# Four-layer linear and segmented attention on one core: the order of the opening, of G's first columns and of the first query loads of each A layer

## The chip, the core and the metric

One NeuronCore of a Trainium2 chip. Its engines run their own instruction queues: TensorE (PE; its weight loads are shown as PEld), VectorE (DVE), ScalarE (ACT), GpSimd (POOL) and SyncE (SP, which here only issues DMAs). The metric is the device time of one execution in microseconds (us); several executions give a median.

## The reference

The input x has 2048 rows of 640 columns (32 heads of 20). Four layers, A, B, A, B, each add to x what they make of its layer norm:

```
A:  q, k, v = x @ wqkv;  pq, pk = phi(q), phi(k)      # phi(t) = t+1 if t>0 else exp(t), + 1e-6
    kv = sum_s pk v^T;  z = sum_s pk                  # per head
    o = (pq kv) / (pq z + 1e-6);  out = o @ wo
B:  four segments of 512 rows, per head: causal softmax attention in the segment,
    mixed by a gate with a read of the memory M, z that the earlier segments left
    out = o @ wo
```

Both A layers use the same weights, and so do both B layers. Everything is float32; the kernel gets it from float16 products by splitting each operand into a high and a low float16 part (three matmuls for each product: high x high, high x low, low x high).

## The kernel before, in words

The 2048 rows go in four segments of 512, each of four tiles of 128 rows; columns go in five chunks of 128 or two halves of 320.

**An A layer in two passes.** The first pass (`g_first`, line 518) goes over the four segments. For each tile it makes the keys (`keys`, line 526: two halves, each 15 matmuls of line 396, then the activation of lines 408 to 411, then two parts at lines 533 and 534 as the tile `pk`), the queries (`queries`, line 542, stored to DRAM as `pqd` by line 546), and, per segment, `memory` (line 549), which adds G = xn^T phi(k): ten products (two halves of columns, five chunks c), each of 12 matmuls of line 560 over the four tiles, evacuated at lines 565 or 567. In segment 0 of the first A layer all keys come first, then memory, then all queries; elsewhere keys and queries alternate.

The last segment ends in `merge` (line 591). It makes the denominators: z summed over partitions by a product with a tile of ones (`square`, line 608; product line 612), `zb` (613) and its reciprocal `rz` (614). It scales G by them (lines 626 to 631), multiplies by the value weight into five tiles `kt` (lines 636 to 657), and these by the output weight into one matrix `wm` (lines 666 to 687). Only then `L["zb"]` is set (between the two, line 661), on which `a_head` (line 714) waits.

The second pass takes three query tiles back at its head: `p_read` (line 697) loads a tile from DRAM (line 701, on SP's queue), multiplies it by `zb` on POOL (703), sums it per head on DVE (706 to 708), scales it on POOL (709). `turn` (line 313) then transposes the tile on PE (320) and copies its high part on ACT (324) and its low part on DVE (325). `a_second` (line 725) multiplies the result by `wm` (line 396 from `o_half`, 465), adds x (`xo`) and feeds the B layer.

**Weights.** `w_prep` (line 228) loads a weight in five chunks into a stage tile (two of these), takes maxima of each chunk on DVE (240), joins them (245, PE 249, 251, PE 255, 258 to 261) into a power-of-two scale, and splits the weight (ACT 265, DVE 266). The query weight's maxima are queued on DVE behind the last lower part that `turn` has issued (`issue_after(self.lower.ins)`).

**The opening** (`opening`, line 1070) starts the first A layer. It normalizes and transposes tile 0, prepares the key weight, then weaves `g_first` with a list of other work: three steps of that list behind each step of segment 0, two behind each step of the later ones. In segment 0 the list is: `others` (transposes of tiles 1 to 3, then their `parts`, line 476), three steps of the query weight, 14 empty steps, the rest of the query weight, and `norms` for segment 1 (its loads, moments and, in `g_norms`, its normalization and eight transposing steps). In segment 1 come the norms of segment 2, then the value and output weights.

**What sets the order.** PE's instructions are issued in the order of the program. Those of the other engines are put in order by a list scheduler, which prefers program order but lets an instruction go ahead when it deems it ready and its engine free; `issue_after` and `high_priority` are the program's means against that. `pause(n)` is n empty steps in a woven list.

**Buffers.** `row` (11 slots of 128 x 640 float32) holds x tiles, normalized tiles, `pk`, `rz`, `kt`, the query tiles read back (`pqi`), their transposes, `xo` and `xn`. There are eight PSUM banks (`bank`).

## Time and profile before

| | |
|---|---|
| median of 3 runs | 1730.26 us (1729.33 to 1732.8) |
| the profiled execution | 1731.61 us, span 1729.8 us |
| PE, DVE, ACT, POOL busy | 95%, 72%, 58%, 31% of the span |
| granted PE clock, mean | 0.992 |
| DMA | 190.89 MB, 110 GB/s over the span |

How to read the profile's lines. A line of the timeline gives the start and the time from first start to last end in us, the engine, the line of the kernel, the operation, the tile written and those read, the shape, the number of instructions merged, and in brackets how long the engine was idle before and who ended it. PE's matmuls overlap each other. A line of the waits gives who waited for whom, the total in us, how often, and the longest. A line of the windows gives a stretch and, for each engine, its busy time and number of instructions, then the granted PE clock as a share of full speed, the busy share of the 16 DMA engines, and GB/s. A line of the chain in order of time gives start, length, and what the time was spent on.

### The profile page before, as it was taken

The numbers are of one execution on the slowest core, as the hardware profiler recorded it, in microseconds if no ns is written. First come the engines' busy times: TensorE is split into PE (matmuls) and PEld (weight loads), VectorE is DVE, ScalarE is ACT, GpSimd is POOL, SyncE is SP. The second block draws the span as 40 slices with busy tenths as digits, with TensorE's granted clock in tenths as the row PEclk, the third lists the DMA queues.
The fourth block names the chain that finished last, engine by engine and source line by source line (L and its number), as shares of the span: only waits on it lengthen the run. The fifth ranks groups of instructions, "written<-read, shape, count | busy, mean of one in ns | idle before, by whom it ended". The sixth has DMA issues, their size and how long they took to land.

```text
span 1729.8 us, 36293 instructions
## 1 busy us (share of the span) xinstructions
PE 1649.9 (95%) x13032; PEld 1032.5 (60%) x13032; DVE 1249.1 (72%) x3966; ACT 997.0 (58%) x1883; POOL 539.3 (31%) x1059
## 2 busy tenths in 40 slices
PE   6999999999999999999999999899999999999998
PEld 4677756554565566556556777566546545645555
DVE  7878785487787677768864457646777877878773
ACT  5666443356657646667675544333675576676673
POOL 3542224032223432333351300321422432233452
PEclk9999999999999999999999999899999999999999
DMA  6424663422322332362211312523232323223432
GB/s 215 141 92 156 220 235 115 137 93 73 105 71 75 104 113 66 124 202 63 82 44 55 99 36 96 199 98 117 73 100 87 113 78 112 94 82 112 133 113 93
DMA packets 110365, 190.89 MB, mean 110 GB/s; under 512 B 14172, under 2 KB 69596, under 8 KB 107624
## 3 DMA queue, kind: packets, MB, share of 16 engines
q1 hardware_dynamic: 97704, 142.68, 25.4%
q0 software_dynamic: 3264, 24.91, 4.0%
q10 hardware_dynamic: 9216, 20.98, 3.1%
q8 instruction: 103, 1.69, 0.4%
q14 instruction: 78, 0.64, 0.1%
HBM read 109.32 MB, written 78.64 MB: 109 GB/s over the span
## 4 chain that ended last, share of the span: by engine, by line
PE 73%; DVE 12%; ACT 7%; POOL 3%; issue 2%; DMA 2%; SPq 0%; ACTq 0%; POOLq 0%; DVEq 0%
PE ps L396 31%; PE ps L382 13%; PE ps L996 7%; PE ps L560 5%; PE ps L320 4%; PE ps L969 4%; PE ps L928 3%; ACT pe L973 3%; DVE ps L934 2%; PE ps L447 2%; PE ps L813 2%; PE ps L1009 1%; DVE wmx L240 1%; DMA pqi<-pqd 1%; PE ps L805 1%
## 5 line engine op out<-in xcount | busy, mean ns | idle before, releaser
L934 DVE CUSTOM_DVE_ANT_0 ps<-ps,maskw 128x384 f32<-128x384 f32 (+3 forms) x1024 | 472.6, 518 | 38.4 <-PE ps L928 35.8
L973 ACT ACTIVATE pe<-ps,lsc 128x512 f32<-128x512 f32 x640 | 397.3, 701 | 75.9 <-PE ps L969 74.6
L396 PEld LDWEIGHTS <-xT 128*128 128x128 f16 x2880 | 281.0, 98 | 112.6 <-issue 7.5
L980 POOL TENSOR_SCALAR_AFFINE_SELECT pe<-pe 128x256 f32<-128x256 f32 (+1 forms) x640 | 229.4, 365 | 370.7 <-ACT pe L973 365.1
L396 PEld LDWEIGHTS <-oT 128*128 128x128 f16 x1920 | 186.1, 98 | 79.7 <-issue 6.4
L996 PE MATMUL ps<-pe,v 128*32 128x512 f32 (+3 forms) x2048 | 165.6, 439 | 12.7 <-POOL pe L980 7.3
L396 PE MATMUL ps<-w_Ak,xT 128*128 128x320 f16 x960 | 140.9, 304 | 2.7 <-ACT w_Ak L265 1.5
L396 PE MATMUL ps<-wm,oT 128*128 128x320 f16 x960 | 142.3, 301 | 1.0
L382 PE MATMUL ps<-xT,w_Bq 128*128 128x512 f16 x600 | 140.3, 379 | 2.8 <-ACT r L420 1.6
L396 PE MATMUL ps<-w_Bo,oT 128*128 128x320 f16 x960 | 141.2, 299 | 1.7 <-ACT oT L324 1.0
L934 DVE DVE_READ_ACCUMULATOR2_ANT mg<- 128x1 f32 x1024 | 142.5, 139 | 0.0
L560 PE MATMUL ps<-pk,xs 128*128 128x321 f16 (+1 forms) x960 | 139.1, 302 | 2.5 <-ACT pk L533 1.6
L382 PE MATMUL ps<-xT,w_Bk 128*128 128x512 f16 x600 | 140.0, 383 | 1.2 <-ACT pe L973 1.2
L396 PE MATMUL ps<-w_Bv,xT 128*128 128x320 f16 x960 | 139.6, 299 | 0.6 <-DVE otok L1016 0.6
L396 PE MATMUL ps<-w_Aq,xT 128*128 128x320 f16 x960 | 137.8, 299 | 0.1
L928 PE MATMUL ps<-ks,qs 60*128 60x512 f16 (+3 forms) x1024 | 122.7, 298 | 6.8 <-ACT pe L973 3.3
L560 PEld LDWEIGHTS <-xs 128*128 128x128 f16 x960 | 93.3, 98 | 40.9 <-issue 3.0
L778 DVE SCALAR_TENSOR_TENSOR nat<-ps,nat 128x512 f16<-128x512 f32 x80 | 55.1, 689 | 82.7 <-ACT nat L777 82.2
L996 PEld LDWEIGHTS ps<-pe,v 128*32 128x32 f32 x2048 | 65.8, 110 | 75.1 <-issue 39.6
L969 PE MATMUL ps<-qs,ks 62*128 62x512 f16 (+3 forms) x1024 | 106.4, 300 | 2.2 <-ACT pe L973 1.1
L411 DVE SCALAR_TENSOR_TENSOR e<-e,r 128x320 f32<-128x320 f32 x128 | 67.7, 529 | 53.1 <-ACT r L410 52.6
L777 ACT ACTIVATE nat<-ps 128x512 f16<-128x512 f32 x80 | 48.4, 606 | 88.0 <-PE ps L382 71.8
(197 smaller groups left out, 2417.7 us busy)
## 6 DMA issues: line engine op xcount, KB each, us to landing
x<-xn ACTq DMA_DIRECT2D x48, 320.0 KB
qs<-qd SPq DMA_DIRECT2D x128, 120.0 KB
ks<-kd SPq DMA_DIRECT2D x128, 120.0 KB
xo<-x SPq DMA_DIRECT2D x48, 320.0 KB
pqi<-pqd SPq DMA_DIRECT2D x32, 320.0 KB
qd<-nat SPq DMA_DIRECT2D x40, 256.0 KB
kd<-nat SPq DMA_DIRECT2D x40, 256.0 KB
x<-in_A_x SPq DMA_DIRECT2D x16, 320.0 KB
```

Of the source, the lines that this page charges most:

```text
L320: nc.tensor.transpose(pt[:, (c - c0) * P:(c - c0 + 1) * P], src[:, c * P:(c + 1) * P], self.ident)
L382: nc.tensor.matmul(p, w[:, c, a, t * P:(t + 1) * P], xT[:, c, b, :], start=k == 0, stop=k == 3 * C - 1)
L396: nc.tensor.matmul(p, xT[:, c, a, i * P:(i + 1) * P], w[:, c, b, n * HN:(n + 1) * HN], start=k == 0, stop=k == 3 * C - 1)
L411: nc.vector.scalar_tensor_tensor(e, e, 1.0, r, op0=OP.min, op1=OP.add)
L560: nc.tensor.matmul(p, xs[:, i, a, c * P:(c + 1) * P], pk[i][:, b, cols], start=k == 0, stop=k == 3 * NT - 1)
L778: nc.vector.scalar_tensor_tensor(nat[:, 1], p, QK_SHIFT, nat[:, 0], op0=OP.mult, op1=OP.subtract)
L928: nc.tensor.matmul(bs[par][:, a:a + n], qs[r, p, i * P:(i + 1) * P], ks[r, p, :n], start=True, stop=True)
L934: nc.vector.tensor_tensor_reduce(bs[par][:, a:a + n], bs[par][:, a:a + n], self.maskw[:, SEG - n:], 1.0, NEG, OP.add, OP.max, G["mg"][:, p ...
L969: nc.tensor.matmul(b[:, a:a + n], ks[r, p, j * P:(j + 1) * P], qs[r, p, j * P:], start=True, stop=True)
L973: nc.scalar.activation(e, b, AF.Exp, scale=self.lsc)
L980: nc.gpsimd.affine_select(d, d, pattern=pat, compare_op=OP.is_ge, fill=0.0, base=0, channel_multiplier=-1)
L996: nc.tensor.matmul(G["pv"][32 * h4:32 * h4 + 32, j * P:], v[j][:, h * E1:h * E1 + 32], G.pop((p, par, j)), start=j == 0, stop=j == 2, skip ...
```

## The change

Six edits.

1. The three tiles that `a_head` reads back for segment 0 of an A layer are loaded as soon as `L["zb"]` is set, which is now right behind the scaling of G; a new key `L["kt"]` is set where `zb` was, and the rest of `p_read` still waits for it.
2. The key weight of layer A is split in two halves of columns, the first half of all five chunks first.
3. Three empty steps stand in front of `others`, and one behind tile 1's transposes, so that both halves of tile 0's keys come before tile 1's transposes on PE, and tile 1's keys before tile 2's; the 14 empty steps become 10, and `g_norms` of segment 1 gets four.
4. The value weight's maxima are queued on DVE behind the last key part issued when its preparation starts (`self.keyed`).
5. In segment 0 of the first A layer, the first two products of G take tiles 0 to 2 first, one behind the other, and tile 3 after that.
6. `square` is filled by POOL instead of DVE.

```diff
-    def w_prep(self, key, stage, w, wait=0, behind=False):
+    def w_prep(self, key, stage, w, wait=0, behind=None):
...
-        with self.tc.issue_after(self.lower.ins) if behind else nullcontext():
+        with self.tc.issue_after(behind.ins) if behind else nullcontext():
...
-        for c in range(C):
-            nc.scalar.activation(w[:, c, 0], st[:, c], AF.Copy, scale=scl)
-            self.last = nc.vector.scalar_tensor_tensor(w[:, c, 1], st[:, c], scl, w[:, c, 0],
-                                                       op0=OP.mult, op1=OP.subtract)
-            if c < C - 1:
-                yield 0.0
+        for cols in (slice(0, HN), slice(HN, D)) if key == ("A", "k") else (slice(0, D),):
+            for c in range(C):
+                nc.scalar.activation(w[:, c, 0, cols], st[:, c, cols], AF.Copy, scale=scl)
+                self.last = nc.vector.scalar_tensor_tensor(w[:, c, 1, cols], st[:, c, cols], scl, w[:, c, 0, cols],
+                                                           op0=OP.mult, op1=OP.subtract)
+                if c < C - 1:
+                    yield 0.0
...
-        yield from self.g_norms(s, box)
+        yield from self.g_norms(s, box, 4 if s == 1 else 0)
...
         xh = self.normed(*m[0])
         yield 0.0
+        yield from pause(wait)
...
+        def product(c, n, tiles, p=None):
+            cols = slice(n * (HN + 1), D + 1 if n else HN + 1)
+            if p is None:
+                p = self.bank()[:, :HN + 1 - n]
+            for i in tiles:
+                for a, b in ((0, 0), (0, 1), (1, 0)):
+                    nc.tensor.matmul(p, xs[:, i, a, c * P:(c + 1) * P], pk[i][:, b, cols],
+                                     start=i == 0 and a == b, stop=i == NT - 1 and a == 1)
+            return p
...
+                    if c == 0:
+                        ahead = 2 if L["early"] and s == 0 and n == 0 else 0
+                        ps = [product(c, n, range(NT - 1)) for c in range(ahead)]
+                    if c < ahead:
+                        p = product(c, n, range(NT - 1, NT), ps[c])
+                    else:
+                        p = product(c, n, range(NT))
...
-        nc.vector.memset(square, 1.0)
+        nc.gpsimd.memset(square, 1.0)
...
+        L["zb"] = zb
         for _ in memory:
             pass
         yield from filled(1)
...
-        L["zb"] = zb
+        L["kt"] = True
...
+    def p_load(self, L, s, i):
         pq = self.row("pqi")
         self.q_pqi.dma_start(pq, L["pqd"][s][i])
+        return pq
+
+    def p_read(self, L, s, i, o, pq=None):
+        nc = self.nc
+        if pq is None:
+            pq = self.p_load(L, s, i)
...
-        box.update(o=[], oT=[self.new_oT()])
+        box.update(o=[], oT=[])
+        pq = [None] * 3
+        if L["kt"] is None:
+            pq = [self.p_load(L, s, i) for i in range(3)]
+        while L["kt"] is None:
+            yield 0.0
+        box["oT"].append(self.new_oT())
         for i in range(3):
-            yield from self.p_read(L, s, i, box["o"])
+            yield from self.p_read(L, s, i, box["o"], pq[i])
...
-                                   key == ("A", "q"))
+                                   {("A", "q"): self.lower, ("A", "v"): self.keyed}.get(key))
...
             xh = [first]
+            yield from pause(3)
             for i in range(1, NT):
                 xh.append(self.normed(*m[i - 1]))
                 yield from self.turn(xh[i], cur[1], i)
+                if i == 1:
+                    yield 0.0
...
-                aux = chain(o, islice(q, 3), pause(14), q, self.norms(src, 1, nxt, 6))
+                aux = chain(o, islice(q, 3), pause(10), q, self.norms(src, 1, nxt, 6))
```

More of the change, by code (lines that the diff above doesn't have):

```diff
@@ L496, in load_segment, with g_norms @@
         yield 0.0
-    def g_norms(self, s, box):
+    def g_norms(self, s, box, wait=0):
         m = box[0]
@@ L515, in g_begin @@
         pqd = [self.dr.tile([NT, P, D], F32, name=f"pqd{n}_{s}") for s in range(NSEG)]
-        return dict(z=z, G=None, pqd=pqd, zb=None, wm=None, early=n == 0)
+        return dict(z=z, G=None, pqd=pqd, zb=None, kt=None, wm=None, early=n == 0)
     def g_first(self, s, box, w, L, behind=None):
@@ L555, in memory @@
                 for c in range(C):
-                    p = self.bank()[:, :HN + 1 - n]
-                    k = 0
-                    for i in range(NT):
-                        for a, b in ((0, 0), (0, 1), (1, 0)):
-                            nc.tensor.matmul(p, xs[:, i, a, c * P:(c + 1) * P], pk[i][:, b, cols],
-                                             start=k == 0, stop=k == 3 * NT - 1)
-                            k += 1
+                    if c == 0:
[5 more added lines that the diff above has]
+                        p = product(c, n, range(NT))
                     g = L["G"][c][:, cols]
@@ L695, in masked @@
         return mem
-    def p_read(self, L, s, i, o):
-        nc = self.nc
+    def p_load(self, L, s, i):
         pq = self.row("pqi")
         self.q_pqi.dma_start(pq, L["pqd"][s][i])
+        return pq
[3 more added lines that the diff above has]
+            pq = self.p_load(L, s, i)
         with self.tc.issue_after(L["split"].ins):
@@ L1098, in last @@
             yield 0.0
+        self.lower = self.keyed = None
         cur = [None, self.x_t(), self.xs_t(0)]
```

## The prediction

> **What bounds the kernel now.** I read the page first, for the shares of engines and of the chain that ended last; then TensorE's (PE's) waits by stage; then busy time in windows.
>
> ```profile
> span 1729.8 us, 36293 instructions
> PE 1649.9 (95%) x13032; PEld 1032.5 (60%) x13032; DVE 1249.1 (72%) x3966; ACT 997.0 (58%) x1883; POOL 539.3 (31%) x1059
> PE 73%; DVE 12%; ACT 7%; POOL 3%; issue 2%; DMA 2%; SPq 0%; ACTq 0%; POOLq 0%; DVEq 0%
> ```
>
> PE is idle for only 80 us. The edits lie in three places that hold part of it: the opening (0 to 66 us), the first head (222 to 263) and the second head (1082 to 1114). The windows show whether time won there is kept (stretch, length; PE, PEld, DVE, ACT, POOL busy with counts; granted PE clock, DMA share, GB/s).
>
> ```profile
> 67.00:118.00 51.00, 51.00 (x381) 37.40 (x379) 40.20 (x91) 38.59 (x76) 30.41 (x49) 1.00 0.24 79
> 165.00:214.00 49.00, 49.00 (x360) 34.92 (x358) 37.95 (x76) 26.37 (x49) 11.00 (x15) 1.00 0.53 192
> 1120.00:1147.00 27.00, 27.00 (x206) 20.41 (x205) 16.20 (x42) 9.11 (x20) 9.91 (x9) 1.00 0.26 86
> ```
>
> Behind the opening and behind the second head PE never rests, at full clock, so a gain there shifts all that follows. I count such gains in full.
>
> **The opening.** The keys of segment 0:
>
> ```profile
> 15.84 3.26 DVE L266 SCALAR_TENSOR_TENSOR w_Ak<-stage,scl_Ak,w_Ak 128x640 f16<-128x640 f32 x4
> 16.76 3.09 PE L396 MATMUL ps<-w_Ak,xT 128*128 128x320 f16 x11 [0.50 <-DVE w_Ak L266]
> 23.41 3.73 PE L396 MATMUL ps<-w_Ak,xT 128*128 128x320 f16 x15
> 27.89 12.39 PE L396 MATMUL ps<-w_Ak,xT 128*128 128x320 f16 x90
> 20.00:28.00 8.00, 5.74 (x31) 4.01 (x30) 4.57 (x15) 6.34 (x14) 6.59 (x13) 0.79 0.91 317
> 28.00:40.20 12.20, 12.20 (x92) 8.78 (x90) 12.03 (x22) 7.08 (x17) 4.19 (x5) 1.00 0.47 163
> 40.20:45.50 5.30, 2.89 (x17) 1.63 (x16) 5.30 (x11) 2.95 (x6) 3.17 (x3) 0.89 0.00 0
> ```
>
> The first half key (15 matmuls) crawls behind the weight's split and ends at 19.85; the second starts at 23.41, behind transposes; the other six are the 90. Split in column halves, the five pieces that the first half key needs take DVE 5 x 0.41 instead of 5 x 0.82 (3.26 / 4), and it ends some 2 us sooner. DVE's total stays (at worst each of five extra starts costs 0.1). With three pauses ahead of the transposes the second half follows at once and ends where its weight does, near 20 instead of 27.1. Then tile 1's transposes and their copies, say 3 us; the 90 matmuls start near 23 instead of 27.89 and, with ten transposes (1.1 us) and some waits for copies among them, end near 37.5 instead of 40.28.
>
> But the last two rows say that from 28 on the limit is DVE: 17.33 of 17.50 us busy. Part of that is work that nothing needs yet:
>
> ```profile
> 36.08 0.14 DVE L245 TENSOR_REDUCE wm<-wmx 128x1 f32<-128x5 f32 x1
> 36.14 0.80 DVE L240 TENSOR_REDUCE wmx<-stage 128x1 f32<-128x640 f32 x1
> 37.83 1.53 DVE L240 TENSOR_REDUCE wmx<-stage 128x1 f32<-128x640 f32 x2
> 40.15 1.53 DVE L240 TENSOR_REDUCE wmx<-stage 128x1 f32<-128x640 f32 x2
> 42.67 0.14 DVE L245 TENSOR_REDUCE wm<-wmx 128x1 f32<-128x5 f32 x1
> 43.17 2.17 DVE L534 SCALAR_TENSOR_TENSOR pk<-e,k_scl,pk 128x320 f16<-128x320 f32 x2
> ```
>
> The first L245 closes the maxima of the query weight. The five L240 behind it and the second L245 are the value weight's, whose program place is in segment 1. They are 0.80 + 1.53 + 1.53 + 0.14 = **4.0 us** between the last keys' steps. The edit pins the maxima behind a key of segment 1, where DVE has 10.8 us free of 51 (row 67 to 118). If that cover fails, the value weight's transpose on PE waits, by at most these 4.0.
>
> So the last key part, at 45.3 now, can be ready at 41.3, if PE's last key matmul ends 2.6 us earlier (two ACT reads, L411, L533, L534, about 0.5 each), at 38.7; 37.5 does. DVE's idle time before 28 (row 20 to 28: 8.00 - 4.57 = 3.4 us) may be filled as well, for 0 to 3 us more; I take none.
>
> G then follows.
>
> ```profile
> PE ps L560 <- ACT pk L533: 1.6, 1, 1.6
> PE ps L560 <- DVE pk L534: 0.8, 1, 0.8
> 45.50:54.00 8.50, 7.83 (x49) 5.01 (x48) 7.02 (x17) 3.71 (x5) 0.48 (x1) 0.87 0.06 25
> 61.16 5.07 PE L560 MATMUL ps<-pk,xs 128*128 128x320 f16 x36
> ```
>
> PE does nine matmuls of G, then waits twice for tile 3's parts. With two columns over three tiles it has eighteen ahead of that point: 9 x 0.14 (5.07 / 36) = **1.3 us** moved into the wait, or the wait gone. The idle time also costs clock: 0.87 over 8.5 us is **1.1 us**, saved if PE doesn't stop. A second PSUM bank is held meanwhile, of eight.
>
> The Trainium skill ("TensorE: Matmul & The Clock Gate", Part 1) says that an idle window of about 3.4 us halves the clock and about 3.4 us of steady work restores it. That agrees with the 0.87 here and, below, with 0.50 behind 7.2 us of idle time; by it the order of the opening could as well keep PE cold, which is rival D.
>
> One wait is left ahead of the queries, PE's transposes of segment 1 behind their normalization.
>
> ```profile
> 55.33 0.77 PE L320 MATMUL ps<-ident,xh 128*128 128x128 f32 x5 [2.00 <-ACT xh L369]
> 66.07 16.46 PE L396 MATMUL ps<-w_Aq,xT 128*128 128x320 f16 x120
> ```
>
> PE and DVE both arrive sooner; the four pauses put one and a third columns (12 x 0.14 each, 2.2 us) in front. Between minus 1 and plus 2 us; I take 0, since G's evacuations and the query weight's split still stand ahead of it on DVE. Sum of the opening: 4.0 + 1.3 + 1.1 = **6.4 us**, bounds 2.5 (ACT and DVE hold each other up, and only the two PE terms stay) and 9.
>
> **The second head.**
>
> ```profile
> 1064.13 26.32 SPq L546 DMA_DIRECT2D pqd<-e  x4
> 1090.62 2.16 SPq L701 DMA_DIRECT2D pqi<-pqd  x4
> 1091.13 11.06 DMA pqi<-pqd
> pqd<-e POOLq DMA_DIRECT2D x32, 160.0 KB, 2.5
> L706 DVE TENSOR_REDUCE rca<-pqi x32: 753/808/821, 257.2 to 1437.4; 128x32 f32<-128x640 f32 x32
> 1070.00:1082.00 12.00, 12.00 (x90) 8.54 (x89) 12.00 (x27) 2.53 (x6) 0.16 (x1) 1.00 0.01 1
> 1091.00:1101.00 10.00, 9.71 (x75) 3.91 (x73) 4.79 (x13) 4.61 (x12) 1.25 (x2) 1.00 1.00 406
> PE ps L320 <- POOL pqi L709: 7.2, 1, 7.2
> 1107.90:1110.10 2.20, 2.15 (x9) 1.72 (x10) 0.68 (x2) 0.81 (x2) 2.20 (x2) 0.50 0.94 401
> 1110.10:1113.50 3.40, 3.40 (x17) 2.12 (x16) 1.58 (x3) 0.49 (x1) 1.75 (x2) 0.61 0.32 136
> ```
>
> The query tiles are read back behind the last query store in SP's queue, at 1090.6, just when two weight fetches fill the DMA engines (share 1.00), and take up to 11 us. PE finishes its product at 1100.7 and stands 7.2 us, to 1107.9. The edit lets the loads go once the denominators are there. They depend on nothing but rows of the pool: of 11, four key parts and rz are held, six are free. SP has only a store to wait for, and the DMA engines are idle (share 0.01). So they go between 1069 and 1087, ahead of the fetches, and land in about 3 us each (an estimate: the 160 KB stores took a median of 2.5). POOL then has three multiplications, DVE three sums (0.8 each; it is idle for 5 of the 10 us from 1091), POOL three scalings, all done by 1100. What is late next is the transposed copy: PE's transposes at 1100.7, ACT and DVE about 1 us, partly beside other transposes; I charge 0.9. Gain 7.2 - 0.9, plus the clock: 2.20 x 0.50 + 3.40 x 0.39 = 2.4. **8.7 us**, bounds 5 and 10.
>
> **The first head.**
>
> ```profile
> 245.65 1.81 SPq L701 DMA_DIRECT2D pqi<-pqd  x4
> 252.37 0.62 DVE L656 TENSOR_TENSOR kt<-ke,kt 128x160 f16<-128x160 f32 x1 [2.31 <-ACT kt L655]
> 262.80 0.55 PE L320 MATMUL ps<-ident,pqi 128*128 128x128 f32 x3 [1.06 <-POOL pqi L709]
> PE ps L612 <- DVE square L608: 1.1, 1, 1.1
> 222.00:237.00 15.00, 14.13 (x104) 9.94 (x103) 15.00 (x34) 5.67 (x10) 0.22 (x1) 1.00 0.22 83
> ```
>
> Here DVE sets the pace (15.00 of 15.00). Earlier loads let the three sums fill its 2.31 us gap, so PE's 1.06 wait and some 0.4 ahead of it go: **1.5 us**, bounds -1 and 3. The memset that moves to POOL frees 0.17 us of DVE and lets PE go 1.1 sooner, but DVE is busy then, so that is counted at nothing; POOL, idle there, hides it. Later heads load as before.
>
> **The sum.** 6.4 + 8.7 + 1.5 = 16.6 us. The profiled execution took 1731.6 (span 1729.8 and 1.8 around it), 1.3 above the median of 1730.26; from that median the forecast is **1714 us**.
>
> **Rivals.** A, the opening yields its 2.5: ACT and DVE pass each half key to and fro, in order, and both were busy already (ACT 6.34 of 8.00 from 20 to 28). 1730.3 - 2.5 - 10.2 = 1718. For it: the ten halves of the key weight add starts on ACT; against it: 4.0 us of DVE work leave. B, the sums slip ahead on DVE in the stretch where it is full (1070 to 1082): 3 x (0.8 + 0.5) = 3.9 us late, 1 covered, so the second head yields 5.8 and the first loses 0.5: 1730.3 - 6.4 - 5.8 + 0.5 = 1718.6. Against it: their program place is still behind the product's inputs. C, the loads stay behind the stores in SP's queue, so the change doesn't do what it says: both heads yield nothing, 1724. With A too, 1728. For it: in the first row of the second head SP sits 26 us on four stores; against it: it does so waiting for data that the loads don't need. D, slower: every gap in the reordered opening keeps PE at half clock. From 21 to 41 some 114 matmuls (90 and the two columns' 24) would take 0.14 more each, 16 us, and the 96 of G behind them 13.4. The opening then loses 29.4 - 6.4 = 23, the heads win 10.2: 1743. If the clock recovers at 41 it is 1730; from about 49 on it is slower than before by over 0.2%. Against it: the stretch from 28 to 40 ran at 1.00 with PE less pressed.
>
> **Chances.** Forecast 0.57, A 0.17, B 0.12, C 0.07, A with C 0.03, D 0.04. Range 1707 (opening 9, second head 10, first 3, and 1 for the spread of runs) to 1723 (A with B); about 0.14 is left out. 0.2% is 3.5 us, about what a measurement of this kernel can tell from no change. Faster by more: the first four, 0.93; within: 0.03; slower: 0.04.
>
> **What would show it.** Right: the value weight's L240 after 80 us; last key part near 41; queries' first matmul near 60 instead of 66.07; pqi loads before the weight fetch, PE's wait for L709 under 1 us, clock 1.00 after it. Wrong: granted clock 0.5 between 25 and 45; DVE sums of pqi before 1082; SP's loads still behind the last store.

## The result and the profile after

Side by side on one chip, the changed kernel took 1722.64 us (median of 5 runs, 1720.99 to 1722.82), the kernel before 1729.33 (1728.34 to 1732.8): ratio 0.9957, 95% interval 0.9942 to 0.9971. On another occasion it took 1721.79 against 1730.68: 0.9954, interval 0.9938 to 0.9970. The change wins 7 to 9 us; the forecast was 16.6. The time lies just inside the forecast's range (1707 to 1723), but that end of it stood for A with B, and B, the late sums of the second head, did not come: that it lies inside is luck.

The page of the changed kernel, span, engines and the chain by engine:

```profile
span 1719.3 us, 36302 instructions
PE 1645.4 (96%) x13032; PEld 1028.9 (60%) x13032; DVE 1250.5 (73%) x3969; ACT 994.2 (58%) x1888; POOL 539.3 (31%) x1061
PE 69%; DVE 15%; ACT 8%; issue 3%; DMA 3%; POOL 2%; SPq 1%; ACTq 0%; DVEq 0%; POOLq 0%
```

PE is idle for 74 us instead of 80, and DVE's share of the chain has risen from 12 to 15%, which points to waits for DVE in place of some of what was won.

I then compared the start of the same matmul in both traces, from the first to the last. PE's lead over the kernel before, in us, in the profiled execution and in that of a repeat (r_after, below):

| place | forecast | measured | repeat |
|---|---|---|---|
| in G, where the kernel before turns to segment 1's transposes (48.7 us) | | 4.4 | 3.6 |
| queries' first matmul (63.4 us) | 6.4 | 2.7 | 1.9 |
| after 150 us | 6.4 | 0.9 | 0.1 |
| behind the first head | 7.9 | 2.4 | 1.7 |
| ahead of the second head (1090 us) | 7.9 | 3.8 | 1.7 |
| behind the second head (1114 us of the kernel before) | 16.6 | 13.0 | 10.8 |
| end | 16.6 | 10.5 | 9.8 |

So the second head gave 9.2 (8.7 forecast). At the first the lead grows by 1.5 and 1.7 (1.5 forecast), but the experiments don't bear this out as the work of edit 1. Of the opening's 6.4, 0.9 and 0.1 were left at 150 us. What else comes and goes, after the heads, are mostly lulls at half clock, told of at the end.

The second head in the changed kernel: SP's and PE's rows, then windows.

```profile
1062.75 1.35 SPq L712 DMA_DIRECT2D pqi<-pqd  x3
1084.44 2.78 SPq L548 DMA_DIRECT2D pqd<-e  x2
```
```profile
1096.80 1.09 PE L321 MATMUL ps<-ident,pqi 128*128 128x128 f32 x8
```
```profile
1091.00:1101.00 10.00, 9.82 (x76) 5.19 (x75) 8.34 (x23) 4.45 (x12) 5.83 (x5) 1.00 0.86 316
1101.00:1114.00 13.00, 13.00 (x100) 9.80 (x99) 8.57 (x25) 4.00 (x9) 2.39 (x3) 1.00 0.62 210
```

Three loads go at 1062.75, ahead of the last stores and of the weights (1090.62 before). PE's transposes of `pqi` start at 1096.80 with nothing waited for; between 1000 and 1130 us the profile lists no wait of PE at all. From 1101 to 1114 it is busy for all 13.00 at clock 1.00.

The opening in the changed kernel, DVE and POOL (an idle time and its releaser stand in brackets):

```profile
33.04 1.40 POOL L479 TENSOR_TENSOR xs<-xh,xs 128x640 f16<-128x640 f32 x1
33.05 1.73 DVE L536 SCALAR_TENSOR_TENSOR pk<-e,k_scl,pk 128x320 f16<-128x320 f32 x1
34.70 2.98 DVE L240 TENSOR_REDUCE wmx<-stage 128x1 f32<-128x640 f32 x4
41.99 0.73 DVE L536 SCALAR_TENSOR_TENSOR pk<-e,k_scl,pk 128x320 f16<-128x320 f32 x1 [0.43 <-ACT pk L535]
42.90 0.49 DVE L412 SCALAR_TENSOR_TENSOR e<-e,r 128x320 f32<-128x320 f32 x1 [0.18 <-ACT r L411]
44.02 0.72 DVE L536 SCALAR_TENSOR_TENSOR pk<-e,k_scl,pk 128x320 f16<-128x320 f32 x1 [0.63 <-ACT pk L535]
```

The four L240 are the query weight's; the value weight's are gone from here, to 96 to 109 us. Yet the last key part ends at 44.02 + 0.72 = 44.7 instead of 45.3: 0.6 earlier, not 4. It was not PE that held it back: PE's last key matmul ended at 38.4, before the 38.7 that the forecast asked for. DVE now stands idle between the last steps, waiting for ACT, and one earlier step lasts 1.73 us, beside a subtraction on POOL. Behind that step it is the other way round: the four maxima run in a row, and ACT waits 2.79 us for DVE's next sum (L412):

```profile
38.12 0.56 ACT L535 ACTIVATE pk<-e,k_scl 128x320 f16<-128x320 f32 x1 [2.79 <-DVE e L412]
```

### The profile page after: what moved, and what is told of

It reads as the page before. It is cut to its first block, busy times and chain, and to the rows that moved or that the text cites. A ratio compares the mean times of both kernels' runs of the same rounds, so it can differ in the third digit from the quotient of the medians.

```text
span 1719.3 us, 36302 instructions
## 1 busy us (share of the span) xinstructions
PE 1645.4 (96%) x13032; PEld 1028.9 (60%) x13032; DVE 1250.5 (73%) x3969; ACT 994.2 (58%) x1888; POOL 539.3 (31%) x1061
## 3 DMA queue, kind: packets, MB, share of 16 engines
q8 instruction: 103, 1.69, 0.4%
## 4 chain that ended last, share of the span: by engine, by line
PE 69%; DVE 15%; ACT 8%; issue 3%; DMA 3%; POOL 2%; SPq 1%; ACTq 0%; DVEq 0%; POOLq 0%
PE ps L397 28%; PE ps L383 13%; PE ps L1020 7%; PE ps L557 4%; PE ps L993 4%; PE ps L952 3%; ACT pe L997 3%; PE ps L321 3%; DVE ps L958 2%; PE ps L448 2%; PE ps L837 2%; PE ps L1033 1%; DVE wmx L240 1%; DVE split L267 1%; DVE st L340 1%
## 5 line engine op out<-in xcount | busy, mean ns | idle before, releaser
L557 PE MATMUL ps<-pk,xs 128*128 128x321 f16 (+1 forms) x960 | 138.7, 301 | 1.4 <-DVE pk L536 1.4
L557 PEld LDWEIGHTS <-xs 128*128 128x128 f16 x960 | 93.3, 98 | 39.6 <-POOL z L541 1.8
L412 DVE SCALAR_TENSOR_TENSOR e<-e,r 128x320 f32<-128x320 f32 x128 | 67.8, 530 | 51.0 <-ACT r L411 50.6
```

Source lines behind the costliest of these rows:

```text
L412: nc.vector.scalar_tensor_tensor(e, e, 1.0, r, op0=OP.min, op1=OP.add)
L557: nc.tensor.matmul(p, xs[:, i, a, c * P:(c + 1) * P], pk[i][:, b, cols], start=i == 0 and a == b, stop=i == NT - 1 and a == 1)
```

## The experiments

Fourteen kernels ran, in four lots, each with the kernel before beside it (1730.02 to 1730.68 us). My theory: the heads do what was forecast, and the opening's gain is lost in DVE's queue, first in the keys, then near 149 us. The rival: the opening wins nothing on PE in the first place.

| kernel | median us | ratio to before, interval |
|---|---|---|
| r_after: the change again | 1721.79 | 0.9954 [0.9938, 0.9970] |
| e1_heads: edit 1 alone | 1720.67 | 0.9948 [0.9934, 0.9963] |
| e2_opening: edits 2 to 5 alone | 1730.32 | 0.9999 [0.9989, 1.0008] |
| e6_vmax: edit 4 alone | 1730.69 | 1.0002 [0.9992, 1.0012] |
| e3_square: change without edit 6 | 1722.58 | 0.9952 [0.9936, 0.9967] |
| e8_nopin: change without edit 4's hold | 1720.17 | 0.9942 [0.9928, 0.9956] |
| e4_casts | 1727.34 | 0.9983 [0.9974, 0.9992] |
| e5_parts (leaves work out) | 1718.55 | 0.9931 [0.9917, 0.9945] |
| e7_pins | 1723.07 | 0.9959 [0.9944, 0.9973] |
| e9_late | 1726.74 | 0.9978 [0.9969, 0.9987] |
| e10_round | 1718.56 | 0.9932 [0.9920, 0.9944] |
| e11_both | 1724.37 | 0.9966 [0.9954, 0.9977] |
| e12_roundnp | 1717.17 | 0.9922 [0.9909, 0.9935] |
| e13_rnpsq | 1717.06 | 0.9925 [0.9913, 0.9937] |

### Heads and opening apart

e1_heads is the kernel before with the early loads alone:

```diff
+        if L["kt"] is None:
+            pq = [self.p_load(L, s, i) for i in range(3)]
```

> Only the early loads of the query tiles, on the kernel before. Theory 1 (the two heads give what was worked out, the opening next to nothing): first head 1.5 us, second 9.0, so PE is 10.5 ahead behind the second head and the time is 1718.5 to 1721. Theory 2 (the heads' gain is partly given back later, and the opening carries part of the whole): the time is 1723 to 1725, well above that of the whole change (1722.6).

e2_opening is the change with the loads and the place of `square` put back.

```diff
-        if L["kt"] is None:
-            pq = [self.p_load(L, s, i) for i in range(3)]
...
-        nc.gpsimd.memset(square, 1.0)
+        nc.vector.memset(square, 1.0)
```

> The opening's edits alone (2 to 5), without the early loads and the moved memset. Theory 1 (the gain is eaten where DVE stops in order for the constants that are loaded behind the value weight): PE is some 2.7 us ahead at the first queries, under 1.2 ahead at 160 us, and the time is 1728 to 1729.5. Theory 2 (the gain at the queries is kept): PE is 2.7 ahead from there to the end, 1726.6.

Edit 1 alone is 9.4 us faster than before, the opening's edits alone nothing: 0.2 us slower, between 1.9 faster and 1.4 slower. So the whole measured gain of the change is that of edit 1. In e2's trace PE is 3.2 us ahead at the queries and 1.5 at 189 us: the rival falls, the gain is there and is lost.

The heads in e1's trace: the second gives 9.2, the first takes 0.4 away, while e2_opening, without the early loads, gains 1.2 there. So theory 1 has its time, but its 1.5 for the first head isn't shown. Of PE's waits there, the one for the scaled tiles (first row, the kernel before) is gone in e1_heads, and one for their transposed copy has come (second row); PE's waits for the parts `xT` of the scaled G grew from 1.6 to 2.7.

```profile
PE ps L320 <- POOL pqi L709: 1.5, 2, 1.1
```
```profile
PE ps L396 <- DVE oT L325: 0.9, 1, 0.9
```

### The value weight's maxima alone

```diff
-                                   key == ("A", "q"))
+                                   {("A", "q"): self.lower, ("A", "v"): self.keyed}.get(key))
```

> The kernel before with one part of the change alone: the maxima of the value weight held behind a key of segment 1. If the prediction's term is right (4.0 us of DVE work stand between the last keys' steps), the last key part comes at 41 to 42 us instead of 45.3, and the time falls by 3 to 4. If DVE's steps there end at the pace of what feeds them (PE's last key matmul at 40.28, ACT's copies of it), the last key part moves by no more than 1 us, DVE shows idle time in its place, and the time falls by no more than 1.

The last key part came at 43.1 + 0.7 = 43.8 us, 1.5 earlier than before, and the time did not fall. DVE in e6_vmax:

```profile
39.05 0.72 DVE L534 SCALAR_TENSOR_TENSOR pk<-e,k_scl,pk 128x320 f16<-128x320 f32 x1 [0.64 <-ACT pk L533]
39.96 0.49 DVE L411 SCALAR_TENSOR_TENSOR e<-e,r 128x320 f32<-128x320 f32 x1 [0.18 <-ACT r L410]
41.08 0.72 DVE L534 SCALAR_TENSOR_TENSOR pk<-e,k_scl,pk 128x320 f16<-128x320 f32 x1 [0.63 <-ACT pk L533]
41.99 0.49 DVE L411 SCALAR_TENSOR_TENSOR e<-e,r 128x320 f32<-128x320 f32 x1
43.12 0.72 DVE L534 SCALAR_TENSOR_TENSOR pk<-e,k_scl,pk 128x320 f16<-128x320 f32 x1 [0.23 <-ACT pk L533]
```

and ACT beside it:

```profile
40.48 0.56 ACT L533 ACTIVATE pk<-e,k_scl 128x320 f16<-128x320 f32 x1 [0.64 <-DVE e L411]
40.95 0.51 ACT L408 ACTIVATE e<-ps,inv_Ak 128x320 f32<-128x320 f32 x1
41.36 0.52 ACT L410 ACTIVATE r<-ps,inv_Ak 128x320 f32<-128x320 f32 x1
42.52 0.57 ACT L533 ACTIVATE pk<-e,k_scl 128x320 f16<-128x320 f32 x1 [0.64 <-DVE e L411]
```

This is a round: ACT reads (L408, L410), DVE adds (L411), ACT writes the part (L533), DVE its low part (L534). ACT's next two reads stand behind its L533, and that waits for DVE. So each half key takes 2.03 us (39.05, 41.08, 43.12), and each engine waits for the other. DVE steps that leave such a round become idle time of DVE: it was busy for 17.33 of 17.50 us before, but the maxima filled gaps that would have been there without them. Two executions of one kernel can differ in when the keys start (by 0.8 us between the change and its repeat), so I also count from the start of the first low part on DVE. From there the last key part is ready after 22.8 us in the kernel before (in e1_heads too) and after 21.0 here. So the forecast's 4.0 was worth 1.8 here and, as e8_nopin shows below, 0.5 in the changed kernel.

### POOL beside DVE

e5_parts is the change with the low parts of the normalized tiles of segment 0 filled with zeros, so it leaves out four subtractions on POOL and what they add to G:

```diff
-        self.nc.gpsimd.tensor_tensor(xs[:, i, 1], xh, xs[:, i, 0], op=OP.subtract)
+        if early:
+            self.nc.gpsimd.memset(xs[:, i, 1], 0.0)
+        else:
+            self.nc.gpsimd.tensor_tensor(xs[:, i, 1], xh, xs[:, i, 0], op=OP.subtract)
```

> The whole change, but in segment 0 the low parts of the normalized tiles (line 479) are filled with zeros by POOL instead of being subtracted: that part of the computation is left out. Theory 1 (DVE's two-input steps run slow beside POOL's subtractions, 1.73 us instead of 0.55): the steps of line 536 take under 0.7 each, and the last key part of segment 0 is ready near 42 instead of 44.7. Theory 2 (the loss is ACT and DVE waiting for each other in turn): it stays at 44 or later. The time by theory 1 is 1 to 2.7 below that of the whole change if nothing eats it, the same if the stop for the constants does.

The groups of the keys' low parts between 20 and 45.5 us, in the change and in e5_parts (busy, mean ns, idle before):

```profile
L536 DVE SCALAR_TENSOR_TENSOR pk<-e,k_scl,pk 128x320 f16<-128x320 f32 x8 | 7.5, 952 | 1.1 <-ACT pk L535 1.1
```
```profile
L539 DVE SCALAR_TENSOR_TENSOR pk<-e,k_scl,pk 128x320 f16<-128x320 f32 x8 | 5.3, 678 | 1.1 <-ACT pk L538 1.1
```

Without the subtractions the eight steps cost 2.2 us less, and nearly all of it is two steps that stand beside a subtraction in the change: 1.56 and 1.73 us, here 0.55 each. (In the kernel before the eight cost 5.7; no low part there stands beside a subtraction, so it is the reordered opening that brought them together.) One step still takes 1.16, beside POOL's sum of z. The last key part came at 42.9 and the queries start at 61.54, each 1.8 us earlier than in the change, which is theory 1's side; of PE's lead of 4.5 at the queries, 2.4 is left at 217 us. The Trainium skill ("SBUF — State Buffer", Who interferes with whom) says that a VectorE instruction with two inputs in SBUF and a GpSimd instruction that reads SBUF can't run side by side: the second waits for the first to end. The trace agrees: in the changed kernel's rows POOL starts at 33.04 and ends at 34.44, DVE's 33.05 ends at 34.78, 0.34 behind it.

### The loss at 149 us

In the changed kernel PE has this wait between 100 and 200 us, which the kernel before has not:

```profile
PE ps L397 <- DVE xT L326: 1.3, 1, 1.3
PE ps L255 <- DVE rs L344: 0.2, 1, 0.2
```

The rows of DVE ahead of it, and of SP:

```profile
133.21 0.23 DVE L184 CAST maskw<-cst 128x128 bf16<-128x128 f32 x1 [4.62 <-DMA cst<-in_const]
147.59 1.53 DVE L240 TENSOR_REDUCE wmx<-stage 128x1 f32<-128x640 f32 x2
149.44 0.88 DVE L326 TENSOR_TENSOR xT<-ps,xT 128x256 f16<-128x256 f32 x2
```
```profile
126.03 0.33 SPq L272 DMA_DIRECT2D wd_Av<-split  x1
126.41 0.42 SPq L182 DMA_DIRECT2D cst<-in_const  x1
133.93 2.23 SPq L236 DMA_DIRECT2D stage<-in_B_wv  x5
```

First I took the casts of the constants, for which DVE waits 4.62 us, and put them on POOL:

```diff
-        nc.vector.tensor_copy(self.maskw[:, SEG - P:], t[:, :P])
-        nc.vector.tensor_copy(self.blk, t[:, P:])
+        nc.gpsimd.tensor_copy(self.maskw[:, SEG - P:], t[:, :P])
+        nc.gpsimd.tensor_copy(self.blk, t[:, P:])
```

> The whole change, but the two casts of the late constants (lines 184 and 185) run on POOL, so that DVE doesn't stand for their load. Theory 1: PE's wait of 1.3 us for the lower part of a transposed tile near 148 us goes, PE stays 2.4 or more ahead up to 214 us, and the time is about 1.4 below that of the whole change, 1721.2. Theory 2 (the wait comes from DVE's load of work, not from the stop): the wait stays and the time is 1722.6.

Both theories fell: PE's wait rose to 2.6 us, and DVE stood at the next load instead. The median is 5.5 above r_after's; the profiled execution, itself faster than that median, has PE 1.5 us behind the kernel before at 217 us. The rest isn't explained.

```profile
148.26 1.64 DVE L240 TENSOR_REDUCE wmx<-stage 128x1 f32<-128x640 f32 x2 [2.47 <-DMA stage<-in_B_wq]
150.21 0.88 DVE L326 TENSOR_TENSOR xT<-ps,xT 128x256 f16<-128x256 f32 x2
```

So I took the order: layer B's maxima stand ahead of L326 in DVE's queue. e7_pins holds all later maxima behind the same key.

```diff
-                                   {("A", "q"): self.lower, ("A", "v"): self.keyed}.get(key))
+                                   self.lower if key == ("A", "q") else self.keyed)
```

> The change with the maxima of all later weights held behind the same key of segment 1, by which the maxima of B's value and query weights stand behind the low parts of the transposed tiles in DVE's queue instead of ahead of them. Theory (the opening's lead is eaten at 149 us because those maxima, one of which waits for a DMA that lands near 148 us, stand ahead of a copy that PE needs): the 1.3 us wait at 149 us goes, PE keeps its lead of 2.6 up to 217 us, and the time is 1 to 2 below the changed kernel's. Rival (DVE's work from 133 to 160 us is too much in total, whatever its order): the wait stays at 1 or more, or another wait for DVE of that length takes its place, and the time stays within 0.5.

The wait for L326 went, and another came: PE's scale of a weight, behind maxima that now come late (at 112 to 115 us, with half clock behind it). PE was 2.1 us behind the kernel before at 136 us. This is the rival's other wait; the median is 1.3 above r_after's, with overlapping intervals.

```profile
PE ps L255 <- DVE wm L251: 3.2, 1, 3.2
```

Both misses said that the late weights are one chain, and that the place to look is where it starts. The value weight's low parts on DVE are written to DRAM (`wd_Av`), the constants' load stands behind that write in SP's queue, and their cast frees the stage buffer for layer B's value weight. e8_nopin gives up the hold of edit 4 and keeps the rest:

```diff
-                                   {("A", "q"): self.lower, ("A", "v"): self.keyed}.get(key))
+                                   self.lower if key == ("A", "q") else None)
```

> The change without the part that holds the value weight's maxima behind a key of segment 1. Theory (the maxima, moved to 96 to 109 us, delay the value weight's low parts on DVE, and by that its write to DRAM, the constants' load behind it in SP's queue, and the later weights, so that DVE comes late to a transposed tile at 149 us): the constants' load is issued before 124 us instead of 126.4, and PE's 1.3 us wait at 149 us falls under 0.5; the last key part comes about 1.5 us later than in the changed kernel, the queries' first matmul likewise, and the time stays within 1 of it. Rival (the late weights' chain does not hang on the maxima): the constants' load stays at 126 us or later, the 1.3 stays, and the time rises by 1.5.

```profile
123.50 0.33 SPq L272 DMA_DIRECT2D wd_Av<-split  x1
123.88 0.42 SPq L182 DMA_DIRECT2D cst<-in_const  x1
131.40 2.24 SPq L236 DMA_DIRECT2D stage<-in_B_wv  x5
```

The wait is gone, and PE keeps the lead that it has at the queries: 2.1 us there and 2.1 at 217 us. The median is 1.6 below r_after's, but the intervals overlap. The last key part came at 44.3 + 0.7 = 45.0 us. Counted from the first low part it takes 21.2 us, and 20.7 in all seven profiles that have the change's keys with the hold: 0.5 later, where I had expected 1.5. Over the kernels that leave the order from the queries to 149 us as it is:

| kernel | queries' first matmul | constants' load | between | PE's wait at 149 | PE's lead at 217 us |
|---|---|---|---|---|---|
| before | 66.07 | 125.83 | 59.8 | none | |
| e1_heads | 65.72 | 125.53 | 59.8 | none | 0.4 |
| e8_nopin | 63.97 | 123.88 | 59.9 | none | 2.1 |
| e12_roundnp | 61.52 | 121.30 | 59.8 | none | 4.6 |
| e13_rnpsq | 59.90 | 119.78 | 59.9 | none | 6.1 |
| e6_vmax (held) | 64.33 | 127.39 | 63.1 | 1.3 | 0.0 |
| the change (held) | 63.38 | 126.41 | 63.0 | 1.3 | 0.9 |
| the change again (held) | 64.17 | 127.28 | 63.1 | 1.3 | 0.1 |
| e3_square (held) | 63.19 | 126.22 | 63.0 | 1.3 | 0.9 |
| e2_opening (held) | 62.85 | 125.88 | 63.0 | 1.3 | 1.5 |
| e5_parts (held) | 61.54 | 124.65 | 63.1 | 1.6 | 2.4 |
| e10_round (held) | 60.99 | 124.29 | 63.3 | 1.3 | 3.0 |

With the hold the constants come 63 us behind the queries, without it 60, whatever else is changed. The hold moves the chain by 3.2 us against PE, and PE then stands for it once, near 149 us.

e9_late sets the constants free of that chain instead:

```diff
-                aux = chain(self.norms(src, 2, nxt, 6), a("v"), a("o"), late())
+                aux = chain(self.norms(src, 2, nxt, 6), late(), a("v"), a("o"))
...
+        with self.tc.issue_after(self.keyed.ins):
+            nc.vector.tensor_copy(self.maskw[:, SEG - P:], t[:, :P])
+            nc.vector.tensor_copy(self.blk, t[:, P:])
```

> The change with the constants' load and casts ahead of the value weight's preparation in segment 1, their casts on DVE held behind a key of that segment, so that the load is not behind the value weight's write in SP's queue and the later weights take a stage buffer that frees at about 126 us instead of 133.9. Theory (the chain through the constants' load eats the opening's lead at 149 us): B's value weight is loaded by 128 us instead of 133.9, PE's 1.3 us wait at 149 us falls under 0.5, PE's lead of 2.6 is kept to 217 us, and the time is 1 to 1.7 below the changed kernel's. Rival (DVE's total of work sets the time there): a wait of PE for DVE of 1 us or more stays between 130 and 217 us, and the time stays within 0.5.

The wait at 149 us is gone and B's value weight loads from 128.14 us, as the theory said, but the lead and the time did not come. The output weight of layer A now takes its stage buffer late (its loads go at 96.39 us, in the change near 60), PE waits for its maxima, at 108 to 112 us with half clock from 111, and is 3.9 us behind the kernel before up to 217 us. Its rows, of SP and of PE's waits:

```profile
96.39 2.24 SPq L237 DMA_DIRECT2D stage<-in_A_wo  x5
```
```profile
PE ps L250 <- DVE wm L246: 4.0, 1, 4.0
```

### The keys' round, and both together

e10_round issues each key part one half key later in segment 0, so that ACT's next reads stand ahead of it:

```diff
                 e = self.phi_a(self.proj_n(xT, w("k"), i, n), self.inv["A", "k"])
-                nc.scalar.activation(pk[i][:, 0, c], e, AF.Copy, scale=self.k_scl)
-                self.keyed = nc.vector.scalar_tensor_tensor(pk[i][:, 1, c], e, self.k_scl, pk[i][:, 0, c],
-                                                            op0=OP.mult, op1=OP.subtract)
+                flush()
+                pend.append((pk[i], c, e))
+                if s or not L["early"]:
+                    flush()
```

> The change with the key parts of segment 0 issued one half key later, so that in ACT's queue the two reads of the next half stand ahead of the part that waits for DVE. Theory (in the tail of the keys the limit is a round of ACT, DVE, ACT, DVE, 2.03 us for each half key, with DVE idle 1.2 of it, which is why 4.0 us taken off DVE brought 1.5): the steps between the last key parts fall from 2.03 to about 1.6, the last key part comes 1 to 2 us earlier than 44.0, and the queries' first matmul by about as much; by the loss at 149 us little of it is kept, and the time stays within 1. Rival (DVE's amount of work sets the tail): DVE stays idle no less, or the last key part stays within 0.4.

The last key part came at 42.6 + 0.7 = 43.3, 1.4 earlier than in the change, and the queries at 60.99, 2.4 earlier (2.1 and 3.1 counted from the first low part). ACT's fifth part, the row of the change that waited 2.79 us, in e10_round:

```profile
36.66 0.56 ACT L530 ACTIVATE pk<-e,k_scl 128x320 f16<-128x320 f32 x1 [1.12 <-DVE e L412]
```

The last key part came as I had said, but not by my theory, and the median fell by 3.2 against r_after's, more than the 1 that I had allowed (the intervals just overlap). Counted from the first low part, this fifth part stands at 14.1 us in the change, 12.0 here and 11.4 in e5_parts; from it to the end of the last low part, all three take 6.6 to 6.7. So all that was won in the keys was won ahead of the fifth part. There the low part that took 1.73 us beside the subtraction, in front of the query weight's maxima, now comes behind them and takes 0.54 (the mean of the eight falls from 952 to 738 ns; one still stands beside a subtraction, 1.55). The round of the last parts as a whole got no shorter: the steps between ACT's last four parts are 1.54, 1.69 and 2.13 us, in the change 0.88, 2.40 and 2.02. (The 1.2 us in that expectation is DVE's busy time in a round, 0.72 + 0.49; it is idle for 0.8.) At 149 us 1.3 was lost again, as expected.

e11_both joins e9's and e10's edits, with `square` back on DVE.

```diff
+                flush()
...
+                aux = chain(self.norms(src, 2, nxt, 6), late(), a("v"), a("o"))
...
+        nc.vector.memset(square, 1.0)
```

> The three edits together on the change: the constants ahead of the value weight, the key parts one half later, and the memset of square back on DVE. If each does what its theory says, PE is 4 to 5 us ahead of the kernel before at the queries and keeps 3.5 or more of it to 217 us, the second head gives its 9, and the time is 2 to 4 below the changed kernel's. If the lulls and DVE's load take it back, the time stays within 1 of the changed kernel's.

It missed: PE was 5.8 us ahead at the queries, then waited 4.4 us for the output weight's maxima, as in e9_late, and was 1.2 behind at 136 us.

e12_roundnp joins the two that worked, e10's edit and e8's, and keeps `square` on POOL.

> The change with the key parts of segment 0 issued one half key later and without the hold on the value weight's maxima. Theory (the round and the delayed weights' chain are the whole loss of the opening): the queries' first matmul comes 4 to 5 us earlier than in the kernel before, PE keeps all of it to 217 us (no wait for the transposed tile at 149 us above 0.3), and the time is 4 to 5 below the changed kernel's, near 1717. Rival (a third limit, DVE's load from 67 to 217 us, takes back any lead above 2): the lead at 217 us is again 2 to 3, with a new wait of PE for DVE between, and the time is that of the change with the key parts alone, 1718.6, or above.

PE is 4.6 us ahead at the queries, and 4.6 at 217 us, with no wait for DVE's transposed tile between: the hold is the whole loss between these two points. e13_rnpsq, with the same opening, has 6.2 and 6.1; no half-clock window falls into its G, and one does in e12_roundnp (50.7 us). 1717.17 us is 4.6 below the repeated change; the two intervals (to 0.9935, from 0.9938) don't overlap. And the value weight's maxima are back among the last keys, where nothing is lost by them. DVE in e12_roundnp:

```profile
38.87 0.55 DVE L531 SCALAR_TENSOR_TENSOR pk<-e,k_scl,pk 128x320 f16<-128x320 f32 x1
39.33 0.81 DVE L240 TENSOR_REDUCE wmx<-stage 128x1 f32<-128x640 f32 x1
40.06 0.54 DVE L531 SCALAR_TENSOR_TENSOR pk<-e,k_scl,pk 128x320 f16<-128x320 f32 x1
41.12 0.80 DVE L240 TENSOR_REDUCE wmx<-stage 128x1 f32<-128x640 f32 x1
41.85 0.53 DVE L531 SCALAR_TENSOR_TENSOR pk<-e,k_scl,pk 128x320 f16<-128x320 f32 x1
```

The last key part is done at 42.4 us (44.7 in the changed kernel), with two of the five maxima between these steps and a third just ahead of them, at 37.74.

### The memset, and the change again

```diff
-        nc.gpsimd.memset(square, 1.0)
+        nc.vector.memset(square, 1.0)
```

> The changed kernel again, unedited, as the base for the others and for a second look at its lulls. Theory (the mechanisms give about 7 to 10 us below the kernel before, the half-clock windows scatter it by 2 to 3): a time of 1720 to 1723, the last key part again at 44 to 45 us, the wait of PE's L397 for the low part of the transposed tile (DVE L326) near 149 us again 1.3, and PE's wait for the memset of square (POOL L620) again near 1.9. Rival (the loss at 149 us is chance of one execution): that wait is under 0.5 in this profile.

> The change with the memset of square back on DVE. Theory (the memset on POOL stands behind POOL's work of the first head and costs PE its wait, and the half-clock window at 221 to 224 us hangs on that stop): PE's wait for it falls from 1.9 to about 1.1, and the time falls by 0.5 to 2 against the changed kernel. Rival (DVE is full there, 15.00 of 15.00 us before, so the memset's place makes no difference): the wait for it is replaced by one as long for DVE, and the time stays within 0.5.

> The same with the memset of square back on DVE. Theory: PE's wait for it at the first head falls from 1.4 to 1.9 to about 1, and the time lies 0 to 1 below the one with it on POOL; the spread of the half-clock windows (one or two of them, up to 1.7 us each) may hide that. Rival: no difference, or 1 us above, because DVE is the engine that is full there.

PE's wait for `square`, on POOL in the change (r_after had the same) and on DVE in e3_square:

```profile
PE ps L624 <- POOL square L620: 1.9, 1, 1.9
```
```profile
PE ps L624 <- DVE square L620: 1.0, 1, 1.0
```

The wait is 0.9 shorter on DVE, and in e13_rnpsq 0.7 against 1.9 in e12_roundnp. The time doesn't show it: 1722.58 against 1721.79, 1717.06 against 1717.17. Other waits of the head for DVE (L643, L557) are longer in its place. r_after repeated the change's two waits, 1.3 and 1.9, so neither is chance.

## Why the prediction was wrong

**The second head: right.** 8.7, measured 9.2 in all thirteen profiles with the early loads and -1.0 and 0.2 in the two without them, with each sign as listed: loads ahead of the weights, no wait of PE for the scaled tiles, clock 1.00 behind.

**The first head: not shown.** The change's profile has the 1.5 of the forecast, but that is luck. Edit 1 alone lost 0.4 there, and e2_opening, without it, gained 1.2. The wait of 1.5 for the scaled tiles went, as I had said; but a wait of 0.9 for their transposed copy came, which I charged in the second head and not here, and others for DVE grew. The kernels with the early loads show 0.4 to 2.6 there with `square` on POOL and -0.7 to 0.6 with it on DVE, but the half-clock window of that stretch lies at another place in most of them (245.8 us before, 220.9 after). The two heads together were forecast at 10.2, and edit 1 alone gave 9.4, about what the second head gives.

**The opening: wrong, and it is nearly the whole miss.** Three steps of it failed.

1. "So the last key part, at 45.3 now, can be ready at 41.3": it came at 44.7. The step took DVE's full 17.33 of 17.50 us for the limit and subtracted 4.0. But the limit for the last keys, where the moved maxima had stood, is the round of ACT and DVE, 2.03 us for a half key, and such work fits into DVE's gaps. The same hold was worth 1.8 us of the last key part on the kernel before and 0.5 in the change, counted from the first low part. My rival A had the mechanism ("ACT and DVE pass each half key to and fro"), and I spoke against it with the very 4.0 that this round swallows. Its 2.5 for the opening is near what PE had at the queries, 2.7 and 1.9, but made up otherwise: PE was 4.4 ahead in G and lost 1.7 in step 2. On top of it the new order set two low parts beside POOL's subtractions, 2.2 us, one of them ahead of the query weight's maxima, for which ACT then waited. My own last row of DVE had shown such a meeting: 2.17 us for two low parts that take 0.54 each elsewhere, beside POOL's sums of z (42.69 to 44.99).
2. "Between minus 1 and plus 2 us; I take 0" for PE's wait for segment 1's normalization: G itself was 4.4 us ahead, and 1.7 of that went here. PE waited 3.6 us in three pieces there (at 51.6, 55.6 and 59.5 us) instead of 2.0 in one. I had written that PE and DVE both arrive sooner. ACT did not:

```profile
46.76 3.71 ACT L265 ACTIVATE w_Aq<-stage,scl_Aq 128x640 f16<-128x640 f32 x5 [2.95 <-DVE scl_Aq L261]
```
```profile
47.02 3.71 ACT L266 ACTIVATE w_Aq<-stage,scl_Aq 128x640 f16<-128x640 f32 x5 [3.03 <-DVE scl_Aq L261]
50.63 0.90 ACT L370 ACTIVATE xh<-x,nb,rs 128x640 f32<-128x640 f32 x1
54.58 0.92 ACT L370 ACTIVATE xh<-x,nb,rs 128x640 f32<-128x640 f32 x1 [1.89 <-DVE nb L347]
```

The query weight's split (first row of before, then of the change) starts no sooner, though PE had the product for its scale at 43.5 us instead of 45.5. The scale's steps on DVE stand behind the last key part, 0.6 sooner, and in the change behind two moments of segment 1 as well (0.87 us), which the kernel before does later. The normalized tiles stand behind the split and behind DVE's `nb`.

3. "Behind the opening and behind the second head PE never rests, at full clock, so a gain there shifts all that follows": 1.8 of 2.7 us were given back by 151 us, 0.3 at 115 and 1.5 at 149. PE's windows were full because what it needs came in time; they didn't show how little earlier it came. The cover that I named for the moved maxima, 10.8 us of DVE's free time from 67 to 118, was there. But I priced their delay by the value weight's transpose on PE alone, and not by the chain behind it: low parts, write to DRAM, the constants' load behind that write, a stage buffer, and layer B's maxima in DVE's queue ahead of a copy that PE needs.

G's own terms came: its waits for key parts fell from 2.4 to 1.4 with more of G in front, and no half-clock window falls into G in the change. That one falls there in e8_nopin (53.4 us) and e12_roundnp (50.7), though, makes the 1.1 for the clock partly the luck of an execution. The key weight's halves cost DVE 0.47 us a piece and not 0.41. The memset "counted at nothing" was right in time, by e3_square and e13_rnpsq, but not in the way: POOL did not hide it, and PE's wait for it rose from 1.1 to 1.9 us.

**What stays open.** How much of e10_round's gain in the keys is the order on DVE and how much the subtraction. What the four maxima of the query weight in front of the fifth sum cost the change: no run moved them. What edit 1 does at the first head. And why the opening's gain is 0.9 and 0.1 in two profiles and 0 in the medians: a program's half-clock lulls move between executions of one kernel (the change has one at 1354.1 us in one profile, at 375.6 in the other, at up to 1.7 us each), so it can't be told closer.

## What to carry to other kernels

An engine that is busy all the time in a window need not be the limit, since its queue may hold work that merely fills gaps: before subtracting such work, follow one item through the engines and see whether its steps wait for each other in a round. Work that is moved "to where there is room" takes everything behind it along, so follow its result through buffers, DMA queues and in-order engines to the next point where the busy engine needs it, and compare that arrival with the lead one hopes to keep. And a gain upstream is kept only as far as the next input that hasn't moved with it.

## What the runs showed of the hardware

The granted clock falls to 0.50 for stretches of 3.4 us or a multiple of it (10.2 us from 1102.5 in the kernel before), and by the profile, which models the ends of matmuls, PE was not idle throughout in the 3.4 us ahead of them. Windows of the changed kernel, in pairs:

```profile
217.50:220.90 3.40, 1.46 (x9) 0.88 (x8) 3.13 (x8) 1.64 (x4) 1.64 (x4) 1.00 0.92 293
220.90:224.30 3.40, 3.40 (x13) 1.73 (x12) 3.26 (x5) 0.00 (x0) 0.12 (x1) 0.50 0.97 334
1350.70:1354.10 3.40, 1.34 (x13) 0.29 (x8) 3.40 (x15) 0.00 (x0) 2.84 (x4) 1.00 0.29 93
1354.10:1357.50 3.40, 3.40 (x16) 1.85 (x14) 2.96 (x9) 1.07 (x2) 0.60 (x1) 0.50 0.17 54
```

A stretch of 3.4 us costs up to 3.40 / 2 = 1.7 us. Which lulls are hit differs from kernel to kernel (before at 580.3 and 1225.4 us, the change at 1354.1 and 1661.3) and between executions, so a lead of PE grows or shrinks by 1 to 2 us at places that no edit touches. The Trainium skill ("TensorE: Matmul & The Clock Gate", Part 1) has the window as free-running, not tied to the start of a kernel. The trace agrees with that as far as the same kernel is hit at 1354.1 us in one execution and at 375.6 in another; that an idle window is needed for it, as the forecast quoted the page, is too narrow here, since PE was busy for 1.34 to 1.46 us of the 3.40 ahead.
